# Preparing block one inside block zero's substitution, with two of its products moved from VectorE to GpSimd

## The chip, the core and the metric

One core of a Trainium2 chip. The metric is the device time of the whole kernel in microseconds (us), median of three runs. Engines are named as in the profile: PE is TensorE, DVE is VectorE, ACT is ScalarE, POOL is GpSimd, SP is the queue that issues most DMAs.

## What is computed

Three stages in a row, all in float32:

```python
for t in range(S):                      # RWKV-like recurrence, 4 x 8 heads, S = 768, head_dim 40
    y[:, :, t] = einsum('bhd,bhde->bhe', rt, state)
    Sa = einsum('bhde,bhe->bhd', state, at)
    state = state * wt - einsum('bhd,bhe->bhde', Sa, bt) + einsum('bhd,bhe->bhde', vt, kt)
x = y as (3072, 320)
h = x @ w_in;  x = (max(h, 0) + alpha * min(h, 0)) @ w_out     # 320 -> 2048 -> 320
out = (silu(x @ w_gate) * (x @ w_val)) @ w_out2                # 320 -> 1536 -> 320
```

## The kernel before, in words

The 768 steps are cut into six blocks of 128 steps, each block into four items (one per batch), each item into two chunks of 64 steps. Block m has the items 4m to 4m+3. For each block the recurrence becomes three pieces of work:

- `preps`: for each item, `prep_a` makes running products of the decay by scans on DVE (L545, L551, L552) and multiplies them into `a` (tile `AN`, L559); `prep_b` multiplies them into b and k (tile `kbt`, L572), PE forms all products of the two (L584), ACT copies parts of these into `tt` (L590, L593) and others back into `AN` (L597), where POOL masks them (L598). PE transposes `kbt`, ACT copies that to `KB` (L612, L615).
- `inverse`: a triangular solve on all 128 partitions, the substitution. It begins with a transpose of `tt` (L630), goes through 31 steps of a multiply and a subtract on DVE (L645, L653), and ends with transposes (L656, L658), small matmuls on PE and copies on ACT (L666 to L693).
- `seq`: per item a scan over its two chunks, which passes PE, ACT, DVE and POOL in turn (`zp`, `pp`, `gp`, `yp`, lines 717 to 817) and at its end writes the block's x to the scratch tensor `xd` by DMAs from ACT's queue.

The weights of both MLPs come in a 64-bit form and are narrowed on the chip by `conv` (DMA in, ACT L191 and L192, DVE L193 and L194, ACT L218, POOL L219, DMA out to `wd`). `mlp1(j)` then loads the x of block j from `xd` (`fill_x`), and runs 16 up and down steps over the weights. For block 0 it is done in two halves of 256 columns for its first eight steps, one as soon as items 0 and 1 have been scanned, the other after items 2 and 3. The second MLP runs after all blocks and is bound by PE.

The order on each engine's queue is fixed when the kernel is built, by a scheduler that takes, of the instructions that could run, the one with the lowest priority number. The number counts up as instructions are written; `tc.cur_priority -= n` lifts what follows by n. `drive` interleaves several generators by their shares of progress, each lifted by its own number. `after(ins, g)` puts the instructions of a generator behind one given instruction on that instruction's engine, and `behind` does so with the substitution step written last. At the start the calls are, in this order:

```python
drive((preps(range(B)), B * N_PREP, HP), (take(c1, EC0), EC0 + .1, 0))
drive((inverse(0), N_INV, HP), (take(p1, EP), EP + .1, BP), (take(c1, EC), EC + .1, CP), ...)
p1, c1 = after(mark["inv"], p1), after(mark["inv"], c1)
rest1 = chain(p1, inverse(1))
drive((seq(0, 0), N_SEQ, SP), (seq(1, 1), N_SEQ, SP), (rest1, ...HP2), (take(c1, NC1), ...CP))
```

`p1` is the preparation of block 1 (items 4 to 7), `c1` the narrowing of the first MLP's weights in 32 steps. With EP = 1 one step of `p1` (the scans of item 4) is written with `inverse(0)`; all others stand behind its last subtract on DVE.

Of the kernel before, what the change touches and what calls it, by code (L numbers as in the profile page):

```python
# [18 lines left out]
XPRI = 1000  # L19
# [29 lines left out]
CP = 2000  # L49
# [14 lines left out]
L = 64  # L64
HALF = 32
LOOK = 2
TRB = 5
LATE = 20
XLEAD = 6
# [4 lines left out]
def kernel(  # L74
# [63 lines left out]
    def ago(n):  # L138
        return ups[-n] if len(ups) >= n else None
# [36 lines left out]
    @contextmanager  # L176
    def lifted(n=XPRI):
        tc.cur_priority -= n
        yield
        tc.cur_priority += n  # L180
# [110 lines left out]
        xst = pool.tile([128, n], F32R, tag="xst", name="xst")  # L291
        return xh, xl, xst

    def fill_x(pool, xs, src, c0, c1):
        xh, xl, xst = (x[..., c0:c1] for x in xs)
        for j in range(3):
            xa = pool.tile([128, c1 - c0], F32, tag="xa", name="xa", bufs=XAB[0])
            if j < 2:
                nc.sync.dma_start(out=xa, in_=src[j * 128:j * 128 + 128])
                split(xa, xh[:, j], xl[:, j], nc.vector)  # L300
            else:
                for p in (lo, hi):
                    nc.sync.dma_start(out=xa[p], in_=src[256:DM])
                nc.scalar.copy(out=xst, in_=xa)
                nc.vector.tensor_tensor(out=xst[hi], in0=xa[hi], in1=xst[hi].bitcast(F32), op=ALU.subtract)

# [31 lines left out]
    def mlp1(j, early=0):  # L338
# [15 lines left out]
        seen = set()  # L354
        for f, c0, c1 in plan:
            if not seen & {(c0, c1), (0, half) if early and c0 == 0 else (c0, c1)}:
                with lifted(), held_by(ago(XLEAD) if j == NM - 1 else None):
                    b0, b1 = c0 // TB, c1 // TB
                    fill_x(xp1, xs, xd[j][:, b0:b1].rearrange("f b t -> f (b t)"), c0, c1)
                seen.add((c0, c1))  # L360
                yield
            t = fetch(wp1, 2 * f, True, j, done)
            ps = e1p["psu"].tile([128, c1 - c0], F32, tag="u", name="u")
            done.append(up_mm(ps, t, tuple(x[..., c0:c1] for x in xs)))
            yield
            if len(pend) == (2 if j == NM - 1 else DEP):
                down(*pend.pop(0))
            pend.append((f, c0, c1, *prelu(e1p["gp3"] if j == NM - 1 and fs.index(f) % 3 == 2 else gp1, ps, f, c1 - c0)))
            yield
# [165 lines left out]
    def prep_a(i):  # L535
# [8 lines left out]
        for g in range(2):  # L544
# [11 lines left out]
        nc.scalar.copy(out=wx[:, ::-1, L:L + 1], in_=rest[:, :, L:L + 1])  # L556
        yield
        an = it["AN"] = item_p.tile([128, 2, NSEG, L], F32, tag="AN", name="AN")
        nc.vector.tensor_tensor(  # L559
            out=an, in0=raw["a", rset(i)].rearrange("q h p (c t) -> q h (p c) t", c=CPB),  # L560
            in1=wx[:, ::-1, 0:L].unsqueeze(1).to_broadcast([128, 2, NSEG, L]), op=ALU.mult,
        )
# [3 lines left out]
    def prep_b(i):  # L566
# [2 lines left out]
        an, mc = it["AN"], TT[m % 2]  # L569
        wi = rests[i % 2][:, :, 0:L][:, :, ::-1]  # L570
        kbt = kbt_p.tile([128, NSEG, 2, L], F32, tag="kbt", name="kbt")
        mark["prep"] = nc.vector.tensor_tensor(  # L572
            out=kbt.rearrange("q s j t -> q j s t"),
            in0=raw["bk", rset(i)].rearrange("q j p (c t) -> q j (p c) t", c=CPB),
            in1=wi.unsqueeze(1).to_broadcast([128, 2, NSEG, L]), op=ALU.mult,
# [5 lines left out]
        for g in range(2):  # L581
# [9 lines left out]
            for h, q in ((0, 1), (1, 3)):  # L591
                pr = slice(32 * q, 32 * q + 32)
                nc.scalar.copy(out=mc[pr, gsl, 0:HALF], in_=ps[pr, :, h, HALF:L])  # L593
            for h, pr in ((0, hi), (1, lo)):
                am = an[pr, h, g * SH:g * SH + SH]
                if AMK & (1 if i < B else 2 if i < 2 * B else 4):
                    nc.scalar.copy(out=am, in_=ps[pr, :, h, :])  # L597
                    nc.gpsimd.affine_select(  # L598
                        out=am, in_=am, compare_op=ALU.is_gt, fill=0.0, base=0,
                        pattern=[[0, SH], [1, L]], channel_multiplier=-1,  # L600
                    )
                else:
                    mark["prep"] = nc.vector.tensor_tensor(
                        out=am, in0=ps[pr, :, h, :], in1=mask[pr].unsqueeze(1).to_broadcast([64, SH, L]), op=ALU.mult,
                    )
            yield
        kb = it["KB"] = (item_x if i < XI else item_q).tile([128, NSEG * 2 * D + 64 - D], F32, tag="KB", name="KB")
        nc.gpsimd.memset(kb[:, NSEG * 2 * D:], 0.0)
        for g in range(NSEG // 4):
            ps = bank([128, 4, 2, 64], "kbp", i)  # L610
            for j in range(4):
                nc.tensor.transpose(  # L612
                    ps[:, j].rearrange("p h e -> p (h e)"), kbt[:, 4 * g + j].rearrange("p j t -> p (j t)"), ident
                )
            nc.scalar.copy(  # L615
                out=kb[:, 8 * g * D:8 * (g + 1) * D].rearrange("p (s h e) -> p s h e", h=2, e=D), in_=ps[:, :, :, 0:D]
            )
            yield

    def scr(m, j):  # L620
# [249 lines left out]

    EC0 = 2
    EC = 4
    EP = 1
    BP = 0
    SP = 3000
    p1 = preps(range(B, 2 * B))
    drive((preps(range(B)), B * N_PREP, HP), (take(c1, EC0), EC0 + .1, 0))
# [1 line left out]
    p1, c1 = behind(p1), behind(c1)  # L879
    drive((inverse(0), N_INV, HP), (take(p1, EP), EP + .1, BP), (take(c1, EC), EC + .1, CP), lead=1, engs=G0, lag=LG0, who=W0)  # L880
    p1, c1 = after(mark["inv"], p1), after(mark["inv"], c1)
    rest1 = chain(p1, inverse(1))
    nrest = B * N_PREP - EP + N_INV
    if FA == 0:
        drive(
            *((chain(seq(j, j), seq(j + 2, j)), 2 * N_SEQ, SP) for j in range(2)),
# [3 lines left out]
        )  # L890
    else:
        drive(
            (seq(0, 0), N_SEQ, SP), (seq(1, 1), N_SEQ, SP),
            (take(rest1, int(nrest * RA)) if RA < 1 else rest1, FAC * nrest, HP2),
            (take(c1, NC1), NC1 - EC - EC0, CP),
        )
    boot.close()
    ps1 = ctx.enter_context(ExitStack())
# [215 lines left out]
```

## Time and profile before

| | |
|---|---|
| median of 3 runs | 1230.73 us (1230.57 to 1231.91) |
| profiled execution | 1229.82 us, span of its instructions 1228.1 us |
| PE busy, share of the span | 1095.4 us, 89% |
| DVE busy | 759.5 us, 62% |
| ACT busy | 602.0 us, 49% |
| POOL busy | 287.4 us, 23% |
| mean granted TensorE clock | 0.944 |

Times of rows are us from the first instruction of the span. A row of a timeline gives its start, how long the instruction (or the merged run of instructions, with its count) lasted, the engine, the line, the operation, the tiles written and read, and in brackets the idle time before it and what ended it. The busy shares are those of the whole span; the stretches of the first 200 us differ much from one another.

### The profile page before, as it was taken

To read this page: it belongs to the slowest core of one execution; us is meant where nothing else is said; L and a number is where in the kernel's file an instruction comes from. 1 tells how busy PE (TensorE), PEld (TensorE's weight loads), DVE (VectorE), ACT (ScalarE), POOL (GpSimd) and SP (SyncE) were. 2 spreads that over 40 slices of the span, in tenths; PEclk is the share of its full clock that TensorE was granted. 3 is DMA by queue.
4 is the path that set the end of the run, shared out by engine and by line. 5 is a ranking of instruction groups with operands and counts; after the bars stand their busy time and mean duration, and the time that the engine had idled before them with its cause. 6 is when DMAs were issued, how large, how long until landed. Compare 5 with 4: busy or idle time off the path is not lost. (4 is left out here: it accounts for less than half of the span.)

```text
span 1228.1 us, 24433 instructions
## 1 busy us (share of the span) xinstructions
PE 1095.4 (89%) x9056; PEld 934.2 (76%) x9056; DVE 759.5 (62%) x1624; ACT 602.0 (49%) x1495; POOL 287.4 (23%) x452
## 2 busy tenths in 40 slices
PE   4146687999999898899989999999999999999998
PEld 4145577877878787788777787787788888888887
DVE  7798988598589669949865434879522323223222
ACT  5559568655954665675655433545332323222222
POOL 8335433401212230341354000536300000000000
PEclk9669776988999998999999999999999999999999
DMA  5534688565554534645486464795010101010000
GB/s 146 186 133 147 214 271 288 172 193 171 158 156 135 175 114 145 194 153 154 125 280 210 148 206 138 250 353 164 1 48 1 48 1 48 1 37 13 22 1 22
DMA packets 94885, 166.36 MB, mean 135 GB/s; under 512 B 13232, under 2 KB 43184, under 8 KB 94768
## 3 DMA queue, kind: packets, MB, share of 16 engines
q1 hardware_dynamic: 86608, 160.88, 41.2%
q10 hardware_dynamic: 8160, 3.93, 1.1%
q8 instruction: 72, 1.18, 0.4%
q14 instruction: 45, 0.37, 0.1%
HBM read 136.98 MB, written 27.79 MB: 134 GB/s over the span
## 5 line engine op out<-in xcount | busy, mean ns | idle before, releaser
L218 ACT CAST gh<-g 128x512 fp32r<-128x512 f32 (+1 forms) x176 | 105.5, 600 | 162.8 <-DVE g L1050 116.2
L1050 DVE TENSOR_TENSOR g<-pv,sg 128x512 f32<-128x512 f32 x72 | 49.7, 691 | 206.3 <-PE pv L274 201.3
L219 DVE TENSOR_TENSOR gl<-g,gh 128x512 fp32r<-128x512 f32 (+1 forms) x176 | 121.9, 692 | 85.7 <-ACT gh L218 83.0
L274 PE MATMUL u<-xh,wt 128*128 128x512 f32 (+1 forms) x416 | 149.0, 401 | 13.5 <-DVE g L315 11.2
L315 DVE SCALAR_TENSOR_TENSOR g<-g,neg,u 128x512 f32<-128x512 f32 (+1 forms) x104 | 73.0, 703 | 88.9 <-ACT g L314 88.4
L274 PEld LDWEIGHTS u<-xh,wt 128*128 128x128 f32 x416 | 80.1, 196 | 32.7 <-DVE g L315 14.4
L314 ACT ACTIVATE g<-u 128x512 f32<-128x512 f32 (+1 forms) x104 | 58.6, 564 | 90.4 <-PE u L274 86.1
L274 PE MATMUL pg<-xh,w 128*128 128x512 f32 x288 | 102.6, 394 | 0.3 <-ACT sg L1048 0.3
L1048 ACT ACTIVATE sg<-pg 128x512 f32<-128x512 f32 x72 | 43.0, 598 | 120.6 <-PE pg L274 120.6
L274 PE MATMUL pv<-xh,w 128*128 128x512 f32 x288 | 100.5, 390 | 0.0
L1034 PE MATMUL o<-w,gh 128*128 128x320 f32 x288 | 87.5, 310 | 2.6 <-ACT gh L218 2.6
L1035 PE MATMUL o<-w,gh 128*128 128x320 f32 x288 | 87.8, 309 | 0.0
L281 PE MATMUL d<-gl,wt 128*128 128x512 f32 (+1 forms) x208 | 82.3, 398 | 1.2 <-DVE gl L219 1.2
L740 POOL COPY gs<-raw_v 64x160 f32<-64x160 f32 x96 | 40.8, 425 | 177.3 <-PE yp L797 108.6
L274 PE MATMUL u<-xl,wt 128*128 128x512 f32 (+1 forms) x208 | 80.8, 389 | 0.0
L653 DVE TENSOR_TENSOR la<-la,tmp 128x96 f32<-128x96 f32 (+43 forms) x306 | 79.3, 285 | 2.0
L282 PE MATMUL d<-gh,wt 128*128 128x512 f32 (+1 forms) x208 | 80.1, 387 | 0.0
L645 DVE TENSOR_TENSOR tmp<-la 128x96 f32<-128x96 f32 (+43 forms) x306 | 78.1, 279 | 1.8
L584 PE MATMUL mnp<-AN,kbt 128*128 128x128 f32 x384 | 59.6, 305 | 21.6 <-DVE AN L559 15.2
L598 POOL TENSOR_SCALAR_AFFINE_SELECT AN<-AN 64x256 f32<-64x256 f32 x96 | 52.2, 544 | 111.2 <-ACT AN L597 99.0
L1036 PE MATMUL o<-w,gl 128*128 128x320 f32 x288 | 77.2, 311 | 1.0 <-DVE gl L219 0.9
L280 PE MATMUL d<-gh,wt 128*128 128x512 f32 (+1 forms) x208 | 72.6, 402 | 2.8 <-DMA wt<-wd 2.8
(123 smaller groups left out, 2635.3 us busy)
## 6 DMA issues: line engine op xcount, KB each, us to landing
wt<-wd SPq DMA_DIRECT2D x98, 384.0 KB
wt<-wd SPq DMA_DIRECT2D x98, 320.0 KB
wd<-wc SPq DMA_DIRECT2D x24, 384.0 KB
raw<-in_moe_w_out_dram SPq DMA_DIRECT2D x28, 320.0 KB
raw_bk<-in_bk_dram SPq DMA_DIRECT2D x48, 160.0 KB
wd<-wc SPq DMA_DIRECT2D x20, 320.0 KB
raw<-in_moe_w_in_dram SPq DMA_DIRECT2D x16, 256.0 KB
raw_v<-in_v_dram SPq DMA_DIRECT2D x24, 160.0 KB
```

Source lines behind the costliest of these rows:

```text
L218: nc.scalar.copy(out=h, in_=raw)
L219: eng.tensor_tensor(out=l, in0=raw, in1=h.bitcast(F32), op=ALU.subtract)
L274: last = nc.tensor.matmul(ps, lt, rh, start=(i == 0), stop=(i == len(ops) - 1))
L280: nc.tensor.matmul(ps, wh, gh, start=first, stop=False)
L281: nc.tensor.matmul(ps, wh, gl, start=False, stop=False)
L282: nc.tensor.matmul(ps, wl, gh, start=False, stop=last)
L315: nc.vector.scalar_tensor_tensor(g, g, neg[:, f:f + 1], ps, ALU.mult, ALU.add)
L645: nc.vector.tensor_tensor(out=tv, in0=ml[:, kk + 1:HALF, kk:kk + 1].to_broadcast([128, nr, ns]), in1=tl[:, kk:kk + 1, c0:c0 + ns].to_broad ...
L653: mark["inv"] = nc.vector.tensor_tensor(out=dst, in0=dst, in1=tv, op=ALU.subtract)
L1034: nc.tensor.matmul(ops[q], gh[:, ts], wh, start=first, stop=False)
L1035: nc.tensor.matmul(ops[q], gh[:, ts], wl, start=False, stop=False)
L1036: nc.tensor.matmul(ops[q], gl[:, ts], wh, start=False, stop=last)
```

## The change

- EP goes from 1 to 28: all steps of the preparation of block 1 are written with `inverse(0)`, lifted by BP = 2500 (the substitution: 3000). `inverse(1)` stands behind the last subtract of `inverse(0)`.
- For items 4 to 7 the products `AN` and `kbt` are computed by POOL instead of DVE.
- For items 0 to 3 the copies and masks of `AN` and the transposes and copies to `KB` are put back by 800, so that the copies to `tt` come first.
- `seq(0, 0)` and `seq(1, 1)` are lifted by 6000 instead of 3000, the weights' narrowing beside them by 3500 instead of 2000.
- The loads of block 0's x, both halves, are issued from ACT's queue instead of SP's, and lifted by 6000 instead of 1000.

```diff
+FIRST = 6000
+LATER = 800
-    def fill_x(pool, xs, src, c0, c1):
+    def fill_x(pool, xs, src, c0, c1, eng=nc.sync):
...
-                nc.sync.dma_start(out=xa, in_=src[j * 128:j * 128 + 128])
+                eng.dma_start(out=xa, in_=src[j * 128:j * 128 + 128])
...
-                    nc.sync.dma_start(out=xa[p], in_=src[256:DM])
+                    eng.dma_start(out=xa[p], in_=src[256:DM])
...
-                with lifted(), held_by(ago(XLEAD) if j == NM - 1 else None):
+                with lifted(XPRI if j else FIRST), held_by(ago(XLEAD) if j == NM - 1 else None):
...
-                    fill_x(xp1, xs, xd[j][:, b0:b1].rearrange("f b t -> f (b t)"), c0, c1)
+                    fill_x(xp1, xs, xd[j][:, b0:b1].rearrange("f b t -> f (b t)"), c0, c1, nc.sync if j else nc.scalar)
...
-        nc.vector.tensor_tensor(
+        (nc.gpsimd if B <= i < 2 * B else nc.vector).tensor_tensor(
             out=an, in0=raw["a", rset(i)].rearrange("q h p (c t) -> q h (p c) t", c=CPB),
...
-        mark["prep"] = nc.vector.tensor_tensor(
+        mark["prep"] = (nc.gpsimd if B <= i < 2 * B else nc.vector).tensor_tensor(
             out=kbt.rearrange("q s j t -> q j s t"),
...
+            tc.cur_priority += LATER if i < B else 0
             for h, pr in ((0, hi), (1, lo)):
                 am = an[pr, h, g * SH:g * SH + SH]
...
+            tc.cur_priority -= LATER if i < B else 0
             yield
...
         for g in range(NSEG // 4):
+            tc.cur_priority += LATER if i < B else 0
             ps = bank([128, 4, 2, 64], "kbp", i)
...
+            tc.cur_priority -= LATER if i < B else 0
             yield
...
-    EP = 1
-    BP = 0
+    EP = 28
+    BP = 2500
+    CP1 = 3500
...
-    rest1 = chain(p1, inverse(1))
-    nrest = B * N_PREP - EP + N_INV
+    rest1 = chain(p1, after(mark["inv"], inverse(1)))
+    nrest = N_INV
...
-            (seq(0, 0), N_SEQ, SP), (seq(1, 1), N_SEQ, SP),
+            (seq(0, 0), N_SEQ, FIRST), (seq(1, 1), N_SEQ, FIRST),
             (take(rest1, int(nrest * RA)) if RA < 1 else rest1, FAC * nrest, HP2),
-            (take(c1, NC1), NC1 - EC - EC0, CP),
+            (take(c1, NC1), NC1 - EC - EC0, CP1),
```

## Rows read from the trace of the kernel before

**Rows 1.** Windows by stage: busy us of each engine, granted clock, DMA share, GB/s.

```profile
core 0: us, PE busy (x) PEld busy (x) DVE busy (x) ACT busy (x) POOL busy (x), PEclk, DMA share, GB/s
40.00:78.00 38.00, 1.57 (x58) 1.57 (x60) 35.93 (x108) 11.34 (x29) 7.63 (x11) 0.50 0.48 158
78.00:116.00 38.00, 28.58 (x438) 25.68 (x433) 34.84 (x54) 36.48 (x101) 21.01 (x28) 0.87 0.47 148
116.00:150.00 34.00, 21.67 (x247) 18.25 (x246) 31.07 (x90) 21.02 (x68) 17.32 (x26) 0.80 0.61 196
150.00:188.00 38.00, 28.52 (x320) 25.60 (x322) 34.09 (x97) 22.19 (x66) 11.95 (x22) 0.76 0.86 274
188.00:204.00 16.00, 13.96 (x259) 12.74 (x255) 14.73 (x24) 14.41 (x32) 6.57 (x8) 0.51 0.87 283
...
240.00:870.00 630.00, 597.50 (x5492) 495.98 (x5491) 460.45 (x1037) 344.27 (x862) 172.04 (x263) 0.97 0.56 178
```

**Rows 2.** Timeline of PE around the ends of both substitutions.

```profile
76.43 3.63 PE L666 MATMUL eps<-la,tt 32*32 32x32 f32 x128 [39.93 <-DVE la L656]
...
91.06 1.15 PE L759 MATMUL pp<-tt,zs 128*64 128x64 f32 x32 [0.19 <-ACT tt L693]
...
186.34 3.62 PE L666 MATMUL eps<-la,tt 32*32 32x32 f32 x128 [4.99 <-DVE la L656]
...
203.94 0.39 PE L274 MATMUL u<-xh,wt 128*128 128x256 f32 x1
```

**Rows 3.** Timeline of DVE around and in the first substitution.

```profile
34.50 1.29 DVE L545 TENSOR_TENSOR_SCAN rest<-wseg,first 128x260 f32<-128x260 f32 x2 [2.70 <-ACT wseg L540]
...
36.07 1.24 DVE L552 TENSOR_TENSOR_SCAN Wx<-wseg,first 128x520 f32<-128x520 f32 x1
...
40.58 1.95 DVE L630 STREAM_TRANSPOSE la<-tt 128x1024 f32<-128x1024 f32 x1 [3.14 <-ACT tt L593]
...
44.41 0.36 DVE L645 TENSOR_TENSOR tmp<-la 128x87 f32<-128x87 f32 x2
...
44.69 1.19 DVE L653 TENSOR_TENSOR la<-la,tmp 128x87 f32<-128x87 f32 x2
...
74.37 2.01 DVE L656 STREAM_TRANSPOSE la<-la 128x1024 f32<-128x1024 f32 x1
```

**Rows 4.** Timeline of POOL: two masks, and one subtract of the weights' narrowing.

```profile
38.70 0.89 POOL L598 TENSOR_SCALAR_AFFINE_SELECT AN<-AN 64x256 f32<-64x256 f32 x2 [1.18 <-ACT AN L597]
...
44.68 0.99 POOL L219 TENSOR_TENSOR wc<-wz,wc 128x384 fp32r<-128x384 f32 x1 [2.79 <-ACT wc L218]
```

**Rows 5.** Instructions of lines 559 and 572, 0 to 420 us: ns min/median/max.

```profile
L559 DVE TENSOR_TENSOR AN<-raw_a,Wx x20: 1211/1227/2014, 11.9 to 410.1; 128x1024 f32<-128x1024 f32 x20
...
L572 DVE TENSOR_TENSOR kbt<-raw_bk,rest x19: 1200/1226/1395, 9.3 to 419.5; 128x1024 f32<-128x1024 f32 x19
```

**Rows 6.** Groups of ACT's preparation copies, 0 to 240 us: busy us, mean ns.

```profile
L597 ACT COPY AN<-mnp 64x256 f32<-64x256 f32 x48 | 17.6, 366 | 1.0
L590 ACT COPY tt<-mnp 64x256 f32<-64x256 f32 x48 | 17.5, 366 | 6.7 <-PE mnp L584 6.0
```

**Rows 7.** Timeline of DVE: last results of both scan pairs, x ready.

```profile
130.91 0.41 DVE L809 TENSOR_TENSOR pv<-yp,Wx 128x256 f32<-128x256 f32 x1
...
149.61 0.42 DVE L305 TENSOR_TENSOR xst<-xa,xst 64x256 fp32r<-64x256 f32 x1 [0.97 <-ACT xst L304]
...
171.65 0.42 DVE L809 TENSOR_TENSOR pv<-yp,Wx 128x256 f32<-128x256 f32 x1
...
191.27 0.42 DVE L305 TENSOR_TENSOR xst<-xa,xst 64x256 fp32r<-64x256 f32 x1
```

**Rows 8.** Timeline of SP's queue: issues of block 0's x loads.

```profile
139.24 0.82 SPq L299 DMA_DIRECT2D xa<-xd  x2
...
145.52 1.23 SPq L303 DMA_DIRECT2D xa<-xd  x2
...
185.07 0.59 SPq L303 DMA_DIRECT2D xa<-xd  x1
```

**Rows 9.** Waits of ACT, 78 to 190 us: total, times, longest.

```profile
ACT pv L717 <- DMA xd<-pv: 4.9, 2, 2.5
```

## The prediction

> **What bounds the kernel now.** I read the windows by stage first. From 240 to 870 us PE is busy for 597.50 of 630 us, 95%, at a clock of 0.97; behind that the second MLP runs on PE alone [rows 1]. Nothing of the change touches that work, so it can only begin it earlier or later. The time to win lies ahead: PE is busy for 1.57 of 38 us in the first substitution, and for 28.58 + 21.67 + 28.52 of the next 110 us [rows 1]. PE's own timeline names the hole: it sat idle for 39.93 us until the transpose of the first substitution's result, and for 4.99 us before the second's [rows 2]. The first matmul of the second half of block 0's x starts at 203.94 [rows 2]; with it the saturated stretch begins.
>
> Next, what fills these 200 us. DVE is busy for 35.93 of 38 us in the first substitution and for 34.84 + 31.07 + 34.09 = 100.0 of the 110 us to 188, where the second one ends: it is the bound there. ACT is the second one, but only from 78 to 116 (36.48 of 38), and nearly free in the substitution before (11.34 of 38). POOL has 7.63 of 38 there [rows 1]. So the preparation of block 1, which now stands in 78 to 116, meets two full engines there and would meet one full engine in the substitution.
>
> The timeline inside the substitution holds the number that decides. Two multiplies on 87 columns take 0.36 us; the two subtracts of the same shape right behind them take 1.19, that is 0.83 more [rows 3]. In just that time POOL runs a subtract of 128x384 that lasts 0.99 us [rows 4]. Both engines read two operands from SBUF. A long product on POOL is thus not hidden from DVE: 0.83 of 0.99, or 84% of it, came back as DVE's wait.
>
> **The change part by part.**
>
> *Copies of tt first.* The substitution's first transpose waited 3.14 us on DVE for ACT's last copy [rows 3]. The gain lies between nothing and these 3.1; the banks that the products fill must still be read by the delayed copies too, so I take half, 1.5.
>
> *Scans of items 5 to 7 in the substitution.* Two scans take 1.29 us and the long one 1.24 [rows 3], 2.5 for an item, 7.6 for three (item 4's are already ahead of it). They lengthen the substitution by 7.6 and leave the stretch behind it by as much.
>
> *AN and kbt on POOL.* Eight products of 128x1024 leave DVE, where an undisturbed one takes 1.23 us [rows 5]: 9.8 saved. No such product ran on POOL. By columns from the 384 of [rows 4], one is 0.99 x 1024/384 = 2.64 us (an estimate); 84% of it as DVE's wait is 2.2. Item 4's two need nothing but its scans, which are done at 38, so they can lie under DVE's idle 3.14 us and its transpose of 1.95 us, which reads one operand [rows 3]. Six are left: 13.3 us. The bounds are 0 (they slip into gaps) and 8 x 2.64 = 21.1. I take 13.3, since the row shows such waits and no gap that long.
>
> *Masks of items 4 to 7.* Sixteen of them, 0.89 a pair [rows 4], 7.1 us of POOL; at 84% 6.0 us of DVE's wait, at best 0. They met DVE before as well, in 78 to 116, so the total is unchanged; in the substitution I take half, 3.0.
>
> *End of the first substitution.* Its last but one transpose ended at 74.37 + 2.01 = 76.4 [rows 3]; it moves by -1.5 + 7.6 + 13.3 + 3.0 = +22.4 to 98.8 (bounds: 80.9 and 111.1).
>
> *From there to the scans.* The first matmul of the scans that needs the solve came at 91.06 [rows 2], 14.7 later, with ACT full. Without block 1's copies between, I take 10.7 (0 to 4 less): 109.5. From 91.06 to the last result of items 0 and 1 at 131.32 [rows 7] it took 40.3. The two largest kinds of copies of the preparation are 17.6 + 17.5 us for twelve items [rows 6], 11.7 for four; out of ACT's full stretch, and with the scans lifted to the front, I take 11.7 off: 28.6, and the last result comes at 138.1, 6.8 later than before (0 off would make it 18.5 later).
>
> *x from ACT's queue.* Before, x was split at 150.03, 18.7 after the last result [rows 7]; SP issued the loads only at 139.24 and 145.52 [rows 8]. ACT waited up to 2.5 us for the written x to land [rows 9]; the four issues took 0.82 + 1.23 on SP, and from the last issue's end to the split x it was 3.3 [rows 7, 8]. With 1 us for issuing the writes this is 9. So x of the first half is there at 147.1, 2.9 earlier than before. What stands behind these loads on ACT's queue waits with them, some 4.5 us a half (the casts of the weights, the copies of the next scans); ACT is busy for 21.02 + 22.19 of 72 us there [rows 1], which covers it; uncovered it would cost these 9. The next two items took 40.75 us, from 131.32 to 172.07 [rows 7]; the same again gives 178.9, and x of the second half at 187.9, against 191.69 [rows 7] before, where SP issued its last load at 185.07 [rows 8].
>
> *Second substitution.* DVE is the bound until then, so I add up its time instead of following waits: + 13.3 - 9.8 - 1.5 = +2.0; and of its idle 10.0 us in 78 to 188 [rows 1], which stood behind a full ACT, I take 4 back (0 to 10). That is -2.0: PE's wait for it ends at 184.3 instead of 186.34 [rows 2]. The narrowing raised above it changes its order, not this sum; that costs nothing as long as the sum is what binds.
>
> *What PE gains.* -2.0 from the earlier end. In 188 to 204 PE idled 2.0 us and worked 13.96 us at a granted clock of 0.51 [rows 1], about the lower of its two levels (1.2 of 2.4 GHz), right after its 4.99 us hole [rows 2]; x of the second half now lies ready at the start of that stretch: -2.0 for the idle, -2 for some of the work that the clock stretched. Together -6.
>
> The sum is made against the profiled execution: 1229.8 - 6 = 1223.8; the median is 0.9 above it, so 1224.7, given as 1225.
>
> POOL's multiply in the substitution costs DVE about as much as the row says, and that is the term on which the sign hangs. The Trainium skill goes further (SBUF — State Buffer, section Who interferes with whom): a VectorE instruction with two SBUF inputs and a GpSimd instruction that reads SBUF exclude each other for the whole instruction. The trace agrees in kind, with 0.83 of 0.99 us. By the rule taken to the letter the sum would be that of the first rival below.
>
> **The rivals.**
>
> *POOL's products hold DVE from end to end (slower).* All eight block it for their 2.64 us: 21.1 instead of 13.3. The first substitution ends at 106.6, x of the second half comes at 195.7, 4 later than before, so nothing is won in 188 to 204; DVE's sum is -2.0 + 7.8 = +5.8: 1235.6, median 1236.5. For it: the wait behind POOL [rows 3, 4]. Against it: item 4's products can run before the substitution starts. It turns the sign once the eight cost DVE about 19 us together, 2.4 each, against 13.3.
>
> *No difference.* DVE's idle time isn't won back (+4) and POOL's price is as forecast; the second substitution then ends at +2.0, and the x that comes earlier gives back 2.0: 1230 to 1231. For it: DVE's sum decides until 188, and there the change takes 9.8 off and puts 13.3 on.
>
> *POOL's products slip between.* At a price of nothing the substitution ends at 85.5 and all behind it is 13.3 earlier: 1211. For it: POOL is idle for 30 of 38 us. Against it: the one row that shows the meeting.
>
> **How the numbers follow.** Chances: 0.42 for the forecast (1219 to 1228), 0.28 for the slower rival, 0.18 for no difference, 0.12 for the free products. Under 0.2% (2.5 us) this kernel's measurement can't tell from no change; so faster 0.54, same 0.18, slower 0.28. The range runs from the free products to the slower rival: 1212 to 1237.
>
> **What would show it.** In the changed profile: products of some 2.6 us on POOL between 38 and 75, with DVE instructions of over 2 us instead of 0.3 beside them; the first transpose near 39, the end of the substitution near 99; ACT far from full behind it; x of the halves split near 147 and 188; PE's second wait shorter and the stretch to 204 at a higher clock. The prediction is wrong if DVE's instructions keep their 0.2 to 0.5 us beside the products (then 1211), if the substitution ends beyond 107, or if PE's saturated stretch begins at 204 although both x came earlier.

## The result and the profile after

The changed kernel took 1248.09 us (median of 4 runs, 1246.35 to 1252.48) against 1230.86 us for the kernel before in the same runs: a ratio of 1.0144, with a 95% interval of 1.0117 to 1.0171. It is 17 us slower, and lies above the range of 1212 to 1237. The profiled execution took 1248.18 us with a span of 1246.5 us, 18.4 more than before.

The windows by stage of the changed kernel, with the columns of [rows 1]:

```profile
40.00:78.00 38.00, 15.67 (x72) 14.34 (x72) 37.05 (x74) 20.63 (x58) 26.91 (x26) 0.60 0.51 162
78.00:116.00 38.00, 15.50 (x312) 14.21 (x312) 36.64 (x96) 21.32 (x53) 13.37 (x18) 0.52 0.32 98
116.00:150.00 34.00, 20.51 (x201) 17.18 (x201) 29.65 (x93) 20.04 (x59) 17.93 (x21) 0.68 0.56 178
150.00:188.00 38.00, 29.02 (x497) 25.27 (x498) 28.96 (x57) 30.13 (x83) 15.65 (x26) 0.82 0.68 212
188.00:204.00 16.00, 14.94 (x173) 13.66 (x173) 13.68 (x25) 14.69 (x46) 10.96 (x14) 1.00 0.87 280
240.00:870.00 630.00, 591.10 (x5470) 487.12 (x5469) 441.60 (x1009) 340.46 (x858) 164.21 (x252) 0.98 0.58 180
```

The preparation did move: PE works 15.67 us in the first substitution instead of 1.57, and ACT falls from 36.48 to 21.32 us in 78 to 116. PE's busy time from 40 to 204 is hardly changed in sum (95.6 us against 94.3 from [rows 1]); the work stands in another order. What is new is the last row: in the stretch that was to be untouched, PE is busy for 6.4 us less than before.

The timeline of DVE in the changed kernel, from the first transpose to the last split of block 0's x (to be held against [rows 3] and [rows 7]):

```profile
40.84 1.98 DVE L636 STREAM_TRANSPOSE la<-tt 128x1024 f32<-128x1024 f32 x1 [2.73 <-ACT tt L595]
...
46.49 2.15 DVE L659 TENSOR_TENSOR la<-la,tmp 128x28 f32<-128x28 f32 x1
...
51.22 2.47 DVE L195 SCALAR_TENSOR_TENSOR wy<-raw,wy 128x320 uint32<-128x320 uint32 x1
...
83.28 1.28 DVE L547 TENSOR_TENSOR_SCAN rest<-wseg,first 128x260 f32<-128x260 f32 x2
86.11 1.23 DVE L554 TENSOR_TENSOR_SCAN Wx<-wseg,first 128x520 f32<-128x520 f32 x1
87.75 1.33 DVE L561 TENSOR_TENSOR AN<-raw_a,Wx 128x1024 f32<-128x1024 f32 x1
90.39 1.27 DVE L547 TENSOR_TENSOR_SCAN rest<-wseg,first 128x260 f32<-128x260 f32 x2
100.87 2.01 DVE L662 STREAM_TRANSPOSE la<-la 128x1024 f32<-128x1024 f32 x1
...
153.75 0.41 DVE L815 TENSOR_TENSOR pv<-yp,Wx 128x256 f32<-128x256 f32 x1
159.68 2.01 DVE L662 STREAM_TRANSPOSE la<-la 128x1024 f32<-128x1024 f32 x1
...
171.62 0.42 DVE L307 TENSOR_TENSOR xst<-xa,xst 64x256 fp32r<-64x256 f32 x1 [1.33 <-ACT xst L306]
...
207.15 0.41 DVE L815 TENSOR_TENSOR pv<-yp,Wx 128x256 f32<-128x256 f32 x1
...
223.27 0.42 DVE L307 TENSOR_TENSOR xst<-xa,xst 64x256 fp32r<-64x256 f32 x1
```

And POOL's products that stand beside the second and third of these rows:

```profile
46.34 2.26 POOL L574 TENSOR_TENSOR kbt<-raw_bk,rest 128x1024 f32<-128x1024 f32 x1 [1.59 <-PE mnp L586]
...
51.10 2.24 POOL L561 TENSOR_TENSOR AN<-raw_a,Wx 128x1024 f32<-128x1024 f32 x1 [1.44 <-DVE Wx L554]
```

A subtract on 28 columns lasts 2.15 us beside a product of 2.26. The rows from 83.28 to 90.39 belong to items 8 and 9: the first scans and one product of the third block slipped into the substitution as well, 5.1 us that the forecast did not have. The first substitution ends at 102.9, the scans of items 0 and 1 at 154.2, x of the two halves is split at 172.0 and 223.7 (before 150.0 and 191.7).

The timeline of PE around the ends of the substitutions, against [rows 2]:

```profile
102.94 3.63 PE L672 MATMUL eps<-la,tt 32*32 32x32 f32 x128 [10.80 <-DVE la L662]
...
113.41 1.87 PE L765 MATMUL pp<-tt,zs 128*64 128x64 f32 x30 [1.33 <-POOL wc L221]
...
161.75 3.62 PE L672 MATMUL eps<-la,tt 32*32 32x32 f32 x128 [2.06 <-DVE la L662]
```

The second substitution ends 24.6 us *earlier* than before, the first one 26.5 later. This points at x of block 0, which needs the first substitution and not the second; u_xfree and d_late below test it.

**One view for all kernels.** Block 1's x takes the buffers of block 0's x and so is split only when the first MLP has done its last multiplication with block 0's (it starts at 314.3 in the kernel before). Its row is the next one in the same timeline, and it is used here as a mark. Changed kernel:

```profile
338.41 0.69 DVE L307 TENSOR_TENSOR xst<-xa,xst 64x512 fp32r<-64x512 f32 x1
```

Kernel before:

```profile
317.03 0.69 DVE L305 TENSOR_TENSOR xst<-xa,xst 64x512 fp32r<-64x512 f32 x1
```

It ends at 339.1 against 317.7, 21.4 us later; from there to the end of the span it is 907.4 against 910.4, 3.0 us shorter. 21.4 - 3.0 = 18.4: at the mark the whole lateness is there.

The mark tells that the first MLP runs late; it does not tell where PE loses its time. These are the windows ahead of the mark and behind it, with the columns of [rows 1], kernel before:

```profile
0.00:317.72 317.72, 220.33 (x2619) 192.64 (x2620) 264.82 (x627) 203.09 (x574) 122.00 (x214) 0.82 0.61 192
317.72:1228.10 910.38, 875.10 (x6439) 741.54 (x6437) 494.65 (x997) 398.93 (x922) 165.42 (x238) 0.99 0.37 116
```

and changed kernel:

```profile
0.00:339.10 339.10, 240.28 (x2838) 209.97 (x2838) 277.34 (x635) 223.73 (x636) 156.79 (x242) 0.83 0.60 183
339.10:1246.50 907.40, 863.21 (x6221) 726.91 (x6219) 482.82 (x981) 380.06 (x859) 159.69 (x219) 0.98 0.37 115
```

Ahead of the mark PE idles hardly longer (98.8 us against 97.4); it is busy for 20.0 us more, with 219 matmuls more, which in the kernel before came behind the mark. Behind the mark it has 218 fewer, is busy for 11.9 us less and idles for 44.2 us instead of 35.3. So the work that PE did early is hardly paid back later: the stretch behind is 3.0 us shorter. Of the 18.4 us, 10.3 are idle time of PE, nearly all of it behind the mark, and 8.1 are longer busy time. Why it is so stays open.

The table has the same numbers for every kernel of this study, in the order in which the second half of block 0's x comes (ends of those rows in the profiled execution; the last two columns are the timed runs, and the ratio is to the kernel before timed beside them). One profiled execution need not be typical: u_raise's took 1229.7 us, and its ten ran from 1228.9 to 1242.8.

| kernel | x, 2nd half | block 1's x | from there to the end | median | ratio, 95% interval |
|---|---|---|---|---|---|
| u_xfree | 132.4 | 317.5 | 908.7 | 1227.6 | 0.9969 [0.9949, 0.9989] |
| n_before2 | 190.5 | 315.2 | 909.3 | 1226.5 | 0.9962 [0.9938, 0.9985] |
| o_xact | 191.2 | 316.2 | 910.2 | 1228.5 | 0.9986 [0.9965, 1.0008] |
| before | 191.7 | 317.7 | 910.4 | 1230.7 | 1 |
| n_before3 | 194.9 | 320.4 | 930.9 | 1250.8 | 1.0152 [1.0131, 1.0173] |
| u_both | 203.1 | 321.3 | 917.4 | 1240.9 | 1.0064 [1.0039, 1.0088] |
| o_pool | 203.6 | 328.5 | 917.2 | 1247.0 | 1.0131 [1.0087, 1.0174] |
| n_before | 205.2 | 316.7 | 922.5 | 1240.9 | 1.0088 [1.0058, 1.0117] |
| u_move | 209.0 | 329.2 | 905.8 | 1237.8 | 1.0057 [1.0035, 1.0079] |
| u_raise | 210.7 | 318.2 | 909.8 | 1235.6 | 1.0035 [1.0007, 1.0063] |
| d_late | 219.0 | 338.0 | 899.3 | 1240.3 | 1.0088 [1.0059, 1.0117] |
| u_xlift | 220.8 | 343.4 | 900.3 | 1246.5 | 1.0120 [1.0083, 1.0156] |
| n_after | 222.9 | 341.9 | 904.8 | 1243.8 | 1.0106 [1.0066, 1.0146] |
| changed | 223.7 | 339.1 | 907.4 | 1248.1 | 1.0144 [1.0117, 1.0171] |
| u_xact | 226.0 | 346.6 | 908.5 | 1256.7 | 1.0203 [1.0177, 1.0229] |
| u_hold2 | 226.6 | 351.8 | 906.2 | 1258.6 | 1.0230 [1.0200, 1.0259] |
| o_move | 227.6 | 345.1 | 908.9 | 1253.7 | 1.0188 [1.0155, 1.0221] |
| u_cp | 230.3 | 341.0 | 913.8 | 1253.3 | 1.0192 [1.0170, 1.0214] |
| u_pool | 230.8 | 357.4 | 905.2 | 1260.3 | 1.0226 [1.0185, 1.0267] |
| u_first | 233.9 | 345.6 | 907.1 | 1254.3 | 1.0191 [1.0162, 1.0220] |

### The profile page after: what moved, and what is told of

It reads as the page before. It is cut to its first block, busy times and chain, and to the rows that moved or that the text cites. A ratio compares the mean times of both kernels' runs of the same rounds, so it can differ in the third digit from the quotient of the medians.

```text
span 1246.5 us, 24462 instructions
## 1 busy us (share of the span) xinstructions
PE 1103.5 (89%) x9056; PEld 936.9 (75%) x9056; DVE 760.2 (61%) x1616; ACT 603.8 (48%) x1495; POOL 316.5 (25%) x460
## 4 chain that ended last, share of the span: by engine, by line
PE 39%; DVE 4%; DMA 4%; issue 2%; ACT 1%; POOL 1%; SPq 1%; ACTq 0%; DVEq 0%; POOLq 0%
PE pg L276 10%; PE pv L276 10%; PE u L276 4%; PE o L1043 3%; PE o L1042 3%; PE o L1041 3%; DMA raw<-in_moe_w_gate_dram 1%; PE d L283 1%; PE d L284 1%; PE d L282 1%; DMA raw<-in_moe_w_val_dram 1%; DVE wz L209 1%; DVE wy L208 1%; DVE g L317 1%; DMA wt<-wd 1%
## 5 line engine op out<-in xcount | busy, mean ns | idle before, releaser
L276 PE MATMUL u<-xh,wt 128*128 128x512 f32 (+1 forms) x416 | 147.5, 398 | 21.9 <-DVE g L317 16.0
L586 PE MATMUL mnp<-AN,kbt 128*128 128x128 f32 x384 | 63.6, 323 | 52.6 <-POOL AN L561 22.2
L586 PEld LDWEIGHTS mnp<-AN,kbt 128*128 128x128 f32 x384 | 56.7, 229 | 57.8 <-POOL AN L561 23.1
L651 DVE TENSOR_TENSOR tmp<-la 128x96 f32<-128x96 f32 (+43 forms) x306 | 89.4, 317 | 1.8
L746 POOL COPY gs<-raw_v 64x160 f32<-64x160 f32 x96 | 44.9, 467 | 158.4 <-PE yp L803 59.3
L659 DVE TENSOR_TENSOR la<-la,tmp 128x96 f32<-128x96 f32 (+43 forms) x306 | 82.2, 291 | 1.9
L284 PE MATMUL d<-gh,wt 128*128 128x512 f32 (+1 forms) x208 | 78.5, 380 | 0.0
L601 POOL TENSOR_SCALAR_AFFINE_SELECT AN<-AN 64x256 f32<-64x256 f32 x96 | 50.7, 528 | 105.1 <-ACT AN L600 88.2
```

The lines of the kernel that those rows point to most:

```text
L276: last = nc.tensor.matmul(ps, lt, rh, start=(i == 0), stop=(i == len(ops) - 1))
L284: nc.tensor.matmul(ps, wl, gh, start=False, stop=last)
L586: nc.tensor.matmul(ps[:, s].rearrange("p h t -> p (h t)"), kbt[:, g * SH + s].rearrange("p j t -> p (j t)"), an[:, :, g * SH + s, :],)
L651: nc.vector.tensor_tensor(out=tv, in0=ml[:, kk + 1:HALF, kk:kk + 1].to_broadcast([128, nr, ns]), in1=tl[:, kk:kk + 1, c0:c0 + ns].to_broad ...
L659: mark["inv"] = nc.vector.tensor_tensor(out=dst, in0=dst, in1=tv, op=ALU.subtract)
```

## The experiments

A name with u_ is the changed kernel with a part undone, o_ the kernel before with one part made; the rest is told at its place.

**First group: four parts undone, one at a time.** The theories were: A, POOL's products hold DVE; B, the place of the preparation costs; C, the raises hold the scans; D, x from ScalarE's queue stands in the way.

u_pool, AN and kbt back on DVE:

```diff
-        (nc.gpsimd if B <= i < 2 * B else nc.vector).tensor_tensor(
+        nc.vector.tensor_tensor(
```

> The changed kernel with AN and kbt of items 4 to 7 back on DVE; all else as changed. Theory A (POOL's products hold DVE, and that is the loss): the first substitution ends near 88 instead of 102.9 and the time comes back to 1230 to 1236. Theory B (the place of the preparation is the loss, whoever multiplies): DVE does 8 x 1.23 = 9.8 us itself instead of waiting some 11 us for POOL, so the substitution ends within 3 us of 102.9 and the time stays at 1244 to 1251.

1260.3: without POOL the kernel is 12 us slower, above both ranges. The substitution ends only 2.3 us earlier (100.7), as B had it and not near 88 as A had it. So A is not borne out.

u_move, the preparation behind the first substitution again:

```diff
-    EP = 28
-    BP = 2500
+    EP = 1
+    BP = 0
...
-    rest1 = chain(p1, after(mark["inv"], inverse(1)))
-    nrest = N_INV
+    rest1 = chain(p1, inverse(1))
+    nrest = B * N_PREP - EP + N_INV
```

> The changed kernel with the preparation of block 1 back behind the first substitution (EP = 1, the second substitution behind it), its products still on POOL. Theory A: POOL's products meet DVE's work there as well, so most of the loss stays, 1240 to 1248. Theory B: the first substitution ends near 78 again, and the time is 1228 to 1234.

1237.8, between the two ranges: 10 us come back, seven are left. The first substitution ends at 77.5 and the first matmul of the scans that needs the solve is at 88.2 (before 91.1), but the two scan chunks take 52.2 us (to 140.4).

u_raise, the three raises taken back:

```diff
-            (seq(0, 0), N_SEQ, FIRST), (seq(1, 1), N_SEQ, FIRST),
+            (seq(0, 0), N_SEQ, SP), (seq(1, 1), N_SEQ, SP),
...
-    CP1 = 3500
+    CP1 = 2000
...
-                with lifted(XPRI if j else FIRST), held_by(ago(XLEAD) if j == NM - 1 else None):
+                with lifted(), held_by(ago(XLEAD) if j == NM - 1 else None):
```

> The changed kernel with the old lifts of the first scans, of the narrowing beside them and of block 0's x (3000, 2000, 1000). Theory C (the narrowing, raised, stands in front of the first scans on ACT and holds them with its waits for POOL and DMA): the scans of items 0 and 1 take under 36 us instead of 40.8, and the time falls by 4 to 10 us. Theories A and B: within 3 us of 1248.

1235.6, 12.5 us back, more than C had: the scans of items 0 and 1 take 35.1 us instead of 40.8, as C had it.

u_xact, x by SP's queue:

```diff
-                    fill_x(xp1, xs, xd[j][:, b0:b1].rearrange("f b t -> f (b t)"), c0, c1, nc.sync if j else nc.scalar)
+                    fill_x(xp1, xs, xd[j][:, b0:b1].rearrange("f b t -> f (b t)"), c0, c1)
```

> The changed kernel with block 0's x loaded from SP's queue again, lifted by 6000 as changed. If the loads on ACT's queue hold what stands behind them (the casts, the next scans), the time falls by 3 to 8 us. If they do what the prediction said, x of the halves comes 5 to 9 us later and the time rises by up to 4. Theories A and B alone: within 3 us of 1248.

1256.7, worse by 8.6, and no expectation met: x came 6.5 us earlier in its first half (165.5) and 2.3 later in its second. D, by which the time would fall, is not borne out.

**Second group: one raise at a time, and parts of the change alone.** u_cp sets only CP1 back to 2000, u_first only the scans' raise (as in the diffs above); o_move is u_move's edit turned round on the kernel before, o_xact u_xact's.

> The changed kernel with one lift undone: the narrowing beside the first scans at 2000 again instead of 3500. Theory C (the raised narrowing stands in front of the scans and of the rest on ACT and DVE): the time falls to 1234 to 1240, and items 2 and 3 are scanned by 200 instead of 207.6. Theory D (another lift, that of the first scans or of x, makes the loss): within 3 us of 1248.

> The changed kernel with one lift undone: seq(0, 0) and seq(1, 1) at 3000 again instead of 6000. Theory C: within 3 us of 1248. Theory D, lift of the scans: 1234 to 1240.

> The kernel before with the preparation of block 1 written with the first substitution (EP = 28, BP = 2500, the second substitution behind it) and nothing else changed: products on DVE, old lifts, x from SP. Theory B (the place is the loss): the first substitution ends 22 to 27 us later and the time is 1238 to 1250. Theory E (the place alone costs little, since PE has other work until 240; only the lifts turn it into a loss): 1229 to 1236.

> The kernel before with block 0's x loaded from ACT's queue and nothing else changed. The step of the prediction: x is split 5 to 9 us sooner after the scans (18.7 and 19.6 us before), and the time falls by 2 to 8 us, to 1223 to 1229. Rival (PE has other work, x is not what it waits for): within 2.5 us of 1231.

u_cp 1253.3 and u_first 1254.3, each above both of its ranges: neither raise, undone alone, wins anything. o_move 1253.7, above B's range, with the first substitution 24.1 us later as B had it: the new place alone, without POOL, raises or ACT's queue, costs 23 us. o_xact 1228.5: no difference that can be told, as the rival had it; x came 4.0 us earlier in its first half and at nearly the same time in its second.

**Third group: does it add up, and is it x?** u_both takes the edits of u_move and u_raise together; u_xlift undoes only the raise of x; o_pool puts only the products on POOL. u_xfree reads block 0's x from an input, so it computes something else and only its time counts (besides this line, the form of the loads is fitted to that input):

```diff
-                    fill_x(xp1, xs, xd[j][:, b0:b1].rearrange("f b t -> f (b t)"), c0, c1, nc.sync if j else nc.scalar)
+                    fill_x(xp1, xs, xd[j][:, b0:b1].rearrange("f b t -> f (b t)") if j else r[0].rearrange("b h d p t -> (h d p) b t")[:, b0:b1], c0, c1, nc.sync if j else nc.scalar)
```

> The changed kernel with the place of the preparation and the three raises undone together; left of the change are the two products on POOL, the copies of tt in front and x from ScalarE's queue. If place and raises are two separate costs, they add: 10.3 us (place undone alone) and 12.5 us (raises undone alone) come off 1248.1, so 1222 to 1229, and the split x of block 1 comes near 308 to 318 us. Rival: the parts don't add, since each edit makes a new order of all the queues; then 1230 to 1240, near the 1237.8 of the place undone alone.

> The changed kernel, but block 0's x is read from an input of the same size instead of from the scans' results (the written x of block 0 is not used), so that it waits for no scan; all else is there. Theory P: the end hangs on when block 0's x is ready, by way of block 0's first MLP, after which block 1's x follows at about 910 us ahead of the end in each profile so far. Then the time falls by at least the 17 us of the loss, to 1215 to 1231, with block 1's x before 318. Rival Q: the loss lies in the order of the work behind 240 us, or in PE's work at the lower clock, whatever x does; then it stays at 1240 to 1250.

> The changed kernel with only the raise of block 0's x undone (from 6000 back to 1000). Of the three raises, undone together worth 12.5 us, the other two undone alone gave nothing (1253 and 1254). Theory X: the raised loads and casts of x stand ahead of the scans' copies on ScalarE and hold them while they wait; then 1234 to 1240, scans of items 0 and 1 done near 149 us. Rival: no single raise costs the time, they only work together; then 1246 to 1256.

> The kernel before with only AN and kbt of items 4 to 7 on POOL; the preparation stays behind the first substitution. With the products off DVE the changed kernel was 12 us slower, so theory: POOL's products help in either place, since DVE saves 1.23 us for each and the wait beside a 2.2 us product is at most about 2 us and not always met; 1222 to 1229. Rival: the wait on DVE eats what is saved, 1229 to 1234.

u_both 1240.9, 0.9 above the rival's range: the parts don't add up (10.3 + 12.5 singly, 7.2 together). u_xlift 1246.5, as the rival had it. u_xfree 1227.6: with x at hand the loss of the changed kernel is gone, as theory P had it. But x there came 91 us earlier than in the changed kernel's second half, and block 1's x no earlier than in the kernel before. Its timeline of DVE:

```profile
131.98 0.42 DVE L307 TENSOR_TENSOR xst<-xa,xst 64x256 fp32r<-64x256 f32 x1 [0.18 <-ACT xst L306]
...
316.79 0.69 DVE L307 TENSOR_TENSOR xst<-xa,xst 64x512 fp32r<-64x512 f32 x1
```

So an x that is 59 us earlier than in the kernel before brings block 1's x no earlier there: with x at hand, something else sets it.

o_pool 1247.0, 16 us slower, both expectations missed. In the old place the products stand in front of work that waits for them. The longest of its waits of PE from 90 to 146 us:

```profile
PE mnp L584 <- POOL AN L559: 8.3, 1, 8.3
```

Scans on DVE are held too. Two of one shape, the second beside POOL:

```profile
96.53 1.24 DVE L552 TENSOR_TENSOR_SCAN Wx<-wseg,first 128x520 f32<-128x520 f32 x1
...
102.99 3.86 DVE L552 TENSOR_TENSOR_SCAN Wx<-wseg,first 128x520 f32<-128x520 f32 x1
```

and what POOL runs there, a product and right behind it two subtracts of the narrowing:

```profile
102.89 2.17 POOL L572 TENSOR_TENSOR kbt<-raw_bk,rest 128x1024 f32<-128x1024 f32 x1
105.03 1.93 POOL L219 TENSOR_TENSOR wc<-wz,wc 128x256 fp32r<-128x256 f32 x2
```

The scans of items 0 and 1 took 54.3 us (90.8 to 145.1; before 40.3).

**Fourth group: a late x by itself, and a new order by itself.** d_late is the kernel before, its loads of block 0's x held by steps of the narrowing (`cvs` lists the last instruction of each step, `HX` is 21 for the first half and 29 for the second):

```diff
-                with lifted(), held_by(ago(XLEAD) if j == NM - 1 else None):
+                with lifted(), held_by(ago(XLEAD) if j == NM - 1 else cvs[HX[c0 > 0]] if j == 0 else None):
```

n_before and n_after change one number that decides ties between scans and preparation (in the kernel before it stands for the scans of items 0 to 3, of which the change raises those of items 0 and 1 by 3000):

```diff
-    SP = 3000
+    SP = 3100
```

u_hold2 is the changed kernel with block 2's preparation held behind the first substitution:

```diff
+    inv0 = mark["inv"]
...
-            g.append((chain(preps(range((m + 1) * B, (m + 2) * B)),
+            pn = preps(range((m + 1) * B, (m + 2) * B))
+            g.append((chain(after(inv0, pn) if m == 1 else pn,
```

> The kernel before, with only this changed: the loads of block 0's x wait for later steps of the narrowing (the 22nd for the first half, done at 168.8 us before; the 30th for the second half, done at 207.6), so x is split some 20 to 25 us later, near 172 and 215 to 222, about where the changed kernel has it. Theory P: the late x alone costs most of the 17 us; 1239 to 1250, block 1's x near 328 to 338. Rival: PE has enough other work in that stretch, and what costs in the changed kernel is the rest of its order; then 1229 to 1236.

> The kernel before with one number changed that stands for nothing of the change: the scans of the first block are raised by 3100 instead of 3000. The order of the queues differs in many places. If single changes of order are small beside the effects told of here, 1228 to 1234. Rival: any new order of this kernel moves the time by 5 us or more, and differences of that size between variants belong to no part; then below 1226 or above 1236.

> The changed kernel with the same number changed (3100 instead of 3000; there it stands for the scans of items 2 and 3). If orders matter little by themselves, 1245 to 1251. Rival as for the kernel before: away from 1248 by 5 us or more.

> The changed kernel with the preparation of block 2 held behind the first substitution, into which its first scans and one product had slipped (about 5.5 us of VectorE's time that the forecast had not seen). Theory: the substitution ends 4 to 6 us earlier, near 98, all behind it too, and since a late x is handed on to the end, 1241 to 1245. Rival: what is taken out there comes back behind it on VectorE, which stays full, so x comes no earlier; 1246 to 1252.

d_late 1240.3, inside what theory P expected; x was split 32.2 and 27.3 us late, its first half 10 us later than in the changed kernel. Its timeline of DVE:

```profile
181.76 0.42 DVE L305 TENSOR_TENSOR xst<-xa,xst 64x256 fp32r<-64x256 f32 x1 [1.63 <-ACT xst L304]
...
218.58 0.42 DVE L305 TENSOR_TENSOR xst<-xa,xst 64x256 fp32r<-64x256 f32 x1
...
337.30 0.69 DVE L305 TENSOR_TENSOR xst<-xa,xst 64x512 fp32r<-64x512 f32 x1
...
700.34 0.69 DVE L305 TENSOR_TENSOR xst<-xa,xst 64x512 fp32r<-64x512 f32 x1
```

With the first substitution and the scans as early as before, the late x alone brings block 1's x 20.3 us late, as in the changed kernel. By block 4's x (701.0 against 693.5 before) 12.8 of that were won back; in the changed kernel (708.4) only 6.4. d_late's own order is a new one too, so its 9.9 us is no exact price.

n_before 1240.9: 10 us slower by 100 in one number. n_after 1243.8, 1.2 below the range expected of a small effect, and 4.3 from 1248, where the rival has 5 or more. u_hold2: the substitution ends at 97.9, 5.0 earlier, as the theory said, and the first half's x 14.9 earlier; but the second pair of scans takes 66.0 us (145.4 to 211.4) and the time is 1258.6. Both expectations missed.

**Fifth group: two more such orders.** n_before2 raises the scans of the later blocks by 3100 instead of 3000 (`SQ`), n_before3 those of the first block by 3300 (`SP`).

> The kernel before with another number changed that stands for nothing of the change: the scans of the later blocks are raised by 3100 instead of 3000, so that ties with the preparation are decided otherwise; the first 200 us keep their work. If most new orders of this kernel cost about what the first such trial did (10 us, all of it behind 450 us), 1236 to 1246. Rival: that trial was an unlucky draw; then 1226 to 1234.

> The kernel before with the scans of the first block raised by 3300 instead of 3000 (3100 gave 1240.9). A third order. If most new orders cost some 10 us, 1236 to 1246; rival: 1226 to 1234.

1226.5 and 1250.8, one to each side. All three trial orders of the kernel before have block 1's x within 2.7 us of it; n_before takes 12.1 us longer behind that and n_before3 20.5. Only n_before2's number has nothing to do with the change; the other two lift, among others, scans that the change lifts too, though by 100 and 300 instead of 3000. The timeline of DVE of n_before3, whose lateness grows from 2.7 us at the first of these rows to 21.2 at the last:

```profile
319.69 0.69 DVE L305 TENSOR_TENSOR xst<-xa,xst 64x512 fp32r<-64x512 f32 x1
...
713.99 0.69 DVE L305 TENSOR_TENSOR xst<-xa,xst 64x512 fp32r<-64x512 f32 x1
```

n_before2 is faster than both kernels of the case (0.9962, interval 0.9938 to 0.9985), by one number in the order of the later blocks.

## Why the prediction was wrong, step by step

The forecast failed on the path from the first substitution to the second half of block 0's x: put at 187.9 us, that x came at 223.7. The two steps that failed most are "I take 11.7 off: 28.6" for the scans of items 0 and 1, which took 40.8, and "the same again" for those of items 2 and 3, which took 53.4. With them fails the premise that a later or earlier start is all that can happen to the work behind 240 us.

*Copies of tt first.* Forecast -1.5; the transpose starts at 40.84 instead of 40.58, behind a wait of 2.73 instead of 3.14 us. Nothing was won.

*POOL's products, the term on which the sign was to hang: right.* Six products met DVE, two lay in front of or under the first transpose, as forecast. Each of the six lasts 2.2 to 2.3 us (estimate 2.64). The six DVE instructions beside them are longer than the shortest of their line and shape by 2.0, 2.0, 2.0, 2.0, 1.3 and 1.8: 11.1 us, forecast 13.3. The Trainium skill (SBUF — State Buffer, section Who interferes with whom) says that a VectorE instruction with two SBUF inputs contends with a GpSimd instruction that reads SBUF; the trace agrees (2.15 us beside 2.26).

*Masks.* Beside the masks DVE's instructions lost about 2 us, forecast 3.0.

*End of the first substitution.* Forecast 98.8, measured 102.9. The missing term is the 5.1 us of block 2's scans and product. With the sizes above (0.3 + 7.6 + 11.1 + 2 = 21.0) it makes 26.1 of the 26.5 us. u_hold2 showed it: without them the end is 97.9.

*From there to the scans.* The tail was right, 10.5 us against 10.7. The next step failed: "I take 11.7 off: 28.6". The relief of ACT came as reckoned, but DVE's work stayed. These are the windows of the two pairs of scans, items 0 and 1, then items 2 and 3, kernel before:

```profile
91.06:131.32 40.26, 26.67 (x308) 23.02 (x308) 36.31 (x76) 34.53 (x105) 23.80 (x38) 0.92 0.51 166
131.32:172.07 40.75, 32.06 (x339) 28.22 (x339) 37.26 (x112) 24.07 (x75) 16.74 (x26) 0.79 0.74 227
```

and changed kernel:

```profile
113.41:154.16 40.75, 24.58 (x274) 20.81 (x274) 35.86 (x114) 22.72 (x66) 20.38 (x26) 0.70 0.60 195
154.16:207.56 53.40, 44.96 (x664) 39.60 (x664) 41.72 (x78) 46.17 (x132) 25.23 (x38) 0.87 0.74 233
```

In the first pair ACT works for 22.72 us instead of 34.53, yet the two chunks took 40.8 us (before 40.3): DVE works for 35.86 us against 36.31. The second substitution, started 11.5 us earlier, came beside them. The groups of DVE in the changed kernel from 113 to 154 us:

```profile
L651 DVE TENSOR_TENSOR tmp<-la 128x120 f32<-128x120 f32 (+30 forms) x36 | 11.7, 348 | 0.1
L659 DVE TENSOR_TENSOR la<-la,tmp 128x120 f32<-128x120 f32 (+31 forms) x38 | 10.2, 292 | 0.1
```

That is 21.9 us of the substitution. In the same chunks before, DVE had 8.6 us of it (lines 630, 645 and 653) and 14.2 of the preparation (products 7.6, scans 6.6), 22.8 together. The space that the preparation left was taken by the next work in line. That this kept the chunks long is argued from these groups; no kernel held the second substitution back, and it is not all: u_raise has 21.4 us of the same two lines in its chunks, and they took 35.1. So the raises had a share. With all three gone the chunks were still 6.5 us above the forecast; with one gone at a time they took 38.9 (u_cp), 44.1 (u_first) and 40.9 (u_xlift), so which of them does it stays open. One way in which it happens can be seen: the narrowing waits in front of the scans' copies on ACT. The timeline of ACT in the changed kernel:

```profile
125.01 0.49 ACT L193 ACTIVATE wz<-raw 128x320 f32<-128x320 f32 x1 [2.71 <-POOL wc L221]
...
125.80 0.60 ACT L779 ACTIVATE gs<-pp 64x160 f32<-64x160 f32 x2
```

The scans' activation at 125.80 needs nothing of the weights (PE had written its `pp` by 121.4) but stands behind their 2.71 us of waiting. What they wait for is POOL's slow subtract, shown in the last section.

*The second pair.* "The same again" is the largest miss, 12.7 us. ACT, with 24.07 of 40.75 us before, is busy for 46.17 of 53.40 us. With the second substitution out of the way early, the preparation of block 2 came beside these scans. Two of its groups on ACT from 154.16 to 207.56 us, of which the kernel before has none in its second pair:

```profile
L592 ACT COPY tt<-mnp 64x256 f32<-64x256 f32 x12 | 4.4, 364 | 0.2
L600 ACT COPY AN<-mnp 64x256 f32<-64x256 f32 x10 | 3.7, 366 | 0.2
```

The kernels of the table agree with it in the main: in the eleven that prepare block 1 inside the substitution the second pair takes 48 to 66 us, with ACT busy for 40 to 49; in the nine others 36 to 51 us (51 is n_before, the next 46), with ACT busy for 22 to 31. It is argued all the same: none held block 2's preparation behind the second pair.

*x from ACT's queue.* Forecast 9 us behind the scans, measured 17.8 and 16.1. The misses on the way to the second half's x add up: 4.1 (substitution) - 0.2 (tail) + 12.2 (first pair) + 12.7 (second pair) + 7.1 (x itself) = 35.9, and 223.7 - 187.9 is 35.8. ACT's idle time was said to cover the loads. But ACT, with other copies to make, issued the last ones only 7.5 us behind the last result at 207.56, and then stood still until they landed:

```profile
215.08 1.71 ACTq L305 DMA_DIRECT2D xa<-xd  x2
...
218.26 0.76 ACT L220 CAST xh<-xa 128x256 fp32r<-128x256 f32 x2 [4.04 <-DMA xa<-xd]
```

*Second substitution and what PE gains.* Forecast 184.3, measured 161.7. The sum of DVE's time took the order of its work as given. Before, the scans of items 2 and 3 (done at 172.1) stood ahead of the second substitution's end; in the changed kernel they are done at 207.6, 46 us behind it. What the substitution set free was not what PE lacked. The clock in 188 to 204 rose from 0.51 to 1.00, as hoped for, while in 78 to 150 it fell from 0.87 and 0.80 to 0.52 and 0.68, with PE's 13.1 us less work in 78 to 116. The gain of 6 was counted at the second substitution's end, while x of block 0 came later.

*The premise* "Nothing of the change touches that work, so it can only begin it earlier or later" failed in two ways. A late x is not just a late start: PE takes up other work meanwhile, and what it does early is hardly paid back behind the mark. And the order behind 240 us changes with edits made ahead of it: two of the trial orders took 12 and 21 us longer behind block 1's x, which itself came within 2.7 us of its old time.

What is shown: with block 0's x at hand, the loss of the changed kernel is gone (u_xfree, 20.5 us, against 4.3 by a mere new order in n_after), and a late x alone brings block 1's x 20.3 us late (d_late), against less than 3 by a mere new order. So block 0's x is the way by which the change reaches the first MLP. The table bears it out: the ten kernels whose second half of x came at 219 us or later have block 1's x at 338 or later and are all slower than before, by 9.9 us at least; those with 190 to 211 have it at 315 to 329. Inside this second group the time of x does not set it: o_pool and u_move (203.6 and 209.0) have block 1's x 11 us late, u_raise (210.7) does not.

What stays open: how much of the 17 us the late x costs, and which part costs how much. d_late's 9.9 us is no more than n_before's 10.4, whose block 1's x was not late. The table's fourth column spans 899 to 931 us, and the trial orders show that one number can move it by 20. Differences of 10 us between two variants, u_pool's 12 and u_xact's 9 among them, can therefore not be put down to the part that was undone. Only the new place of the preparation stands out of that, in time barely: made alone it cost 23 us (o_move), and block 1's x came 27 us late. The rival "POOL's products hold DVE from end to end" had the sign right with the wrong mechanism: they held it less than forecast.

## What to carry to other kernels

When work is taken from behind a serial stage into it, ask what the scheduler will put into the place that comes free: here the next substitution took it and finished 25 us early for nobody, the next preparation followed it, and what the long MLP waits for came 32 us late. Find the transfer that the chain of the busiest engine starts from, and follow that through the change, rather than sums of busy time. In a kernel whose queues are ordered by priorities, first time two or three orders that should mean nothing; here they spread over 24 us, more than the change cost.

## What the runs showed of the hardware

A product of 128x1024 takes POOL 2.2 us and DVE 1.23 [rows 5]. It delays not only DVE's multiplies: the scan of 1.24 us took 3.86 beside a product and the two subtracts behind it (o_pool, rows above). A transpose, which reads one operand, was not delayed: 1.98 us beside a product of 2.18 that starts at 40.30 in the changed kernel, against 1.95 in [rows 3].

The blocking goes the other way too. POOL in the changed kernel, beside DVE's stream of the second substitution:

```profile
119.12 5.85 POOL L221 TENSOR_TENSOR wc<-wz,wc 128x256 fp32r<-128x256 f32 x2 [1.72 <-ACT wc L220]
```

DVE has no gap between the rows below, the last of which ends at 124.11; POOL is done 0.9 us later:

```profile
119.01 0.55 DVE L659 TENSOR_TENSOR la<-la,tmp 128x207 f32<-128x207 f32 x2
...
123.77 0.34 DVE L659 TENSOR_TENSOR la<-la,tmp 128x190 f32<-128x190 f32 x1
```

The same two subtracts in o_pool:

```profile
124.62 1.31 POOL L219 TENSOR_TENSOR wc<-wz,wc 128x256 fp32r<-128x256 f32 x2
```

4.5 us more for the same work. The Trainium skill (SBUF — State Buffer, section Who interferes with whom) has it that the order of issue decides who blocks. The 2.15 us subtract agrees with that: it started 0.15 us behind POOL's product. POOL's subtract, however, waited not only for the instruction that had started 0.11 us ahead of it but for the 18 that started behind it as well.
